# One state pair moved to another buffer, three products and one group of output evacuations moved to other places in the order (one core, Trainium2)

## The chip, the cores and the metric

The kernel runs on one core of a Trainium2 chip. A core has a matrix engine (PE, with its own weight-load stream PEld), a vector engine (DVE), a scalar engine (ACT), a general engine (POOL) and an engine that issues transfers (SP). Each takes its instructions in a fixed order and waits on semaphores for the others; transfers run beside them. The metric is the device time of one execution in microseconds (us), the median over several executions. The profile is one execution of its own, with every instruction's start and duration.

## The reference, cut to what matters

`x` is 2048 x 1024. Two branches are computed from it and mixed by a gate per row.

```
a  = S5 branch:  Bu = x B_bar^T (complex, 1024 states); h_t = Lam_bar h_(t-1) + Bu_t;  a = 2 Re(h C^T) + x Dskip
b  = H3 branch:  kv = shiftconv(k) * v;  y = FFT long convolution of kv with ssm_k;  b = x * (y + kv ssm_D)
g  = sigmoid(sum(x * gate_w))
out = g * a + (1 - g) * b
```

## The kernel before, in words

The work has two stages that overlap. In the first, about 215 us long, the convolution of the H3 branch is computed per chunk of 128 channels (eight chunks; loop `for c in range(NC - 1)` and then the last chunk, `c = 7`): tables and forward transforms on PE, products of spectra on DVE (`products`), the inverse on PE (`inverse`). Its results go to a scratch in HBM (`cv_scr`) and are read back by rows later (`loads`).

The second stage is the state recurrence. Time is cut into four blocks (`tb`) of 512 steps and the states into four groups (`g`) of 256. One pair `(tb, g)` is one item of the list `order`. For item `i`:

- `Bu(i)` makes two tiles on PE ("B12" in the plan means both tiles of item 12). ACT moves them from PSUM into a state buffer `U` (the half steps `V_` and `O_`), and writes first the carried end value into it (`U<-ends`).
- `turn_U` (the list `turns_U[i]`) multiplies one half by lambda on ACT (into `Q`), twice, and each time a POOL transfer that adds (`gather`, `U<-Q`) brings it into the other half. The second transfer of an item goes to the same place as the first.
- `scan(tb, g, ...)` is the recurrence on DVE: a front (two products with tables and two sums: `A<-TCS`, `trn<-TCS`, `A<-A,trn`), four scan instructions, then the products back (`U<-TCS,A`, `trn<-TCS,A`) and the join (`U<-U,trn`). Then the state is scaled by lambda, by ACT for the scans in `scaled_by_act = (4, 12, 13, 14)` (put into `put_off` and issued later as four `Q<-U`), by DVE else; the sums of scan j are woven between the scan instructions of scan j+1.

Outputs are made per row tile `k` (16 of 128 rows, four to a block): `Cy_row(k)` ("C0") or, for blocks 1 and 2, in groups: "G23" is group 3 of block 2, 32 matmuls, 8 for each of its four row tiles. Group 0 takes all four PSUM buffers, group 3 ends with `scale_a` (ACT, PSUM into SBUF, scaled by the gate) and `combine` (POOL transfer that adds the other branch). The last block (rows 12 to 15) takes the same four PSUM buffers again after them. `scale_b(k)` prepares the other branch of row `k`: two ACT passes, and a POOL transfer `pbb<-gd` (for some rows called `BT<-gd`, `BT<-BT` or `row<-gd`, after the buffer that they use). `product(k)` multiplies it with x on DVE, and waits for that transfer.

The order of everything is the order of the source text: `put` (L94) chains every instruction behind the previous one of its engine. The driver is the loop `for j in range(NS)` over the 16 scans: `advance(j)` runs scan j and weaves the front of scan j+1 into it; `between(j)` is called inside the scan, ahead of its scan instructions and again after them; then come `turned` (turns), `scaled_b`, and the units of `plan[j]`. All instructions have line L94 in the profile; the tile names tell them apart.

Buffers: `u4` is a pool of three buffers that serves temporaries early and the states 6, 7, 8 and 15 late. `fin` is a region at the right end of SBUF. It holds the temporary `t` of the last chunk's `products`, and was closed again when the last chunk's B tiles had been issued; the matrices `CT[4..7]` then took its place.

Of the kernel before, what the change touches and what calls it, by code (L numbers as in the profile page):

```python
# [11 lines left out]
BF16 = mybir.dt.bfloat16  # L12
# [8 lines left out]
def kernel(  # L21
# [46 lines left out]
    def pool(name, bufs, **kw):  # L68
        return ctx.enter_context(tc.tile_pool(name=name, bufs=bufs, **kw))
# [10 lines left out]
    s5p = {"wu": pool("wu", 3)}  # L80
# [5 lines left out]
    def ps2(shape, name):  # L86
        return psum.tile(shape, F32, name=name, tag="ps")
# [29 lines left out]
    def act(o, i, **kw):  # L117
        put("act", nc.scalar.activation, out=o, in_=i, **kw)

    def load_t(o, i):  # L120
        put("sp", nc.sync.dma_start_transpose, out=o, in_=i)
# [58 lines left out]
    def hold(column):  # L180
        act(column, pih, func=ACT.Copy)
# [74 lines left out]
    def load_xT(tb, halves=(0, 1), held=False):  # L256
        if tb == NTB - 1:
            xTs[tb] = BT[3].rearrange("p c d q -> p (c d q)").rearrange("p (d t) -> p d t", d=ND)
        elif tb not in xTs:
            xTs[tb] = (xt_pool if tb in (1, 2) else xt_first).tile([128, ND, TB], BF16, name="xT", tag="xT")  # L260
        for h in halves:
            if held:
                hold(xTs[tb][:, 0, h * HB:h * HB + 1])
            load_t(xTs[tb][:, :, h * HB:(h + 1) * HB], xf[tb * TB + h:(tb + 1) * TB:2, :])
# [502 lines left out]
    def inverse(c):  # L767

        G = whole.pop(c).rearrange("p (a c b f d) -> p a c b f d", a=2, c=2, b=4, d=128)
        for par in range(2):  # L770
            ps = ps2([128, 2, 4, 128], "psz")
            for j in range(2):
                tl = 2 * par + j
                for fi in range(2):
                    for cc, tab in enumerate((CI, SI)):
                        mm(ps[:, j], tab[:, fi, tl * 128:(tl + 1) * 128], G[:, par, 1 - cc, :, fi],
                           fi == 0 and cc == 0, fi == 1 and cc == 1)
            cv = cv_pool.tile([128, 2, 4, 128], BF16, name="cv")
            act(cv, ps, func=ACT.Copy)
            move(cv_scr[c, :, 2 * par:2 * par + 2], cv)  # L780
            yield
# [16 lines left out]
    def gate(tb):  # L798
        psg = ps2([128, 2, 512], "p")[:, 0, 0:4]
        for tl in range(4):  # L800
            for dt_ in range(ND):
                mm(psg[:, tl:tl + 1], xTs[tb][:, dt_, tl * 128:(tl + 1) * 128], gwb[:, dt_:dt_ + 1],
                   dt_ == 0, dt_ == ND - 1)
        gates_of(slice(tb * 4, tb * 4 + 4), psg)
# [28 lines left out]
    def Bu(i):  # L833
        tb, g = order[i]
        if i == 13:
            V_ = s5p["v13"].tile([128, 2, 2, HB], BF16, name="V13")
            O_ = lam_pool.tile([128, 2, 2, HB + 2], BF16, name="O13", tag="lamd")
            Us[tb, g] = V_, O_[:, :, :, 2:]
            turns_U[i] = turn_U(g, V_, O_)
            return [Bu_plain(tb, g, V_, O_, j) for j in range(2)]  # L840
        if i in (10, 11):
            if i == 10:
                s5p["u2"] = xt_pool.tile([128, 2, 2 * (4 * HB + 4)], BF16, name="U2", tag="xT")
            U = s5p["u2"][:, i - 10]
        else:
            shape = [128, 2 * (4 * HB + 4)]
            if i in (6, 7, 8, 15):
                U = u4(shape, BF16, "U")
            else:
                home = uu[0 if i in (0, 1, 14) else 1] if i < 6 or i == 14 else s5p["uu"]  # L850
                U = home.tile(shape, BF16, name="U")
        if i >= 2:
            V_, O_ = U[:, 0:4 * HB], U[:, 4 * HB:]
            V_ = V_.rearrange("p (c j t) -> p c j t", c=2, j=2)
            O_ = O_.rearrange("p (c j t) -> p c j t", c=2, j=2)
            Us[tb, g] = V_, O_[:, :, :, 2:]
            turns_U[i] = turn_U(g, V_, O_)
            return [(Bu_halves if i < 4 else Bu_plain)(tb, g, V_, O_, j) for j in range(2)]
        U = U[:, 0:8 * HB].rearrange("p (a c j t) -> p a c j t", a=2, c=2, j=2)
        Us[tb, g] = U[:, 0], U[:, 1]  # L860
        return [Bu_tile(tb, g, U, j) for j in range(2)]
# [24 lines left out]
    turns_U = {}  # L886
# [220 lines left out]
    def product(t_):  # L1107
        pbb, xr = ios[t_]
        tt(xr, xr, pbb, ALU.mult)
# [7 lines left out]
    def step(gen):  # L1117
        next(gen, None)

    def run(gen):  # L1120
        for _ in gen:
            pass

    def steps(gen, n):
        for _ in range(n):
            step(gen)
# [55 lines left out]
    old = none  # L1182
    parts = (None for i in range(4) for b in Bu(i) for _ in b)
    tiles = (b for i in (4, 5) for b in Bu(i))

    for c in range(NC - 1):
# [36 lines left out]
        tabs, back, prod = turn_table(c - 1) if c <= NG else none, inverse(c - 1), products(c)  # L1223
# [88 lines left out]
        old = tabs  # L1312

    h3r.close()
    c = NC - 1
# [34 lines left out]
    turning = [turn_C(pi) for pi in range(NP)]  # L1350
    load_CT(1)
    load_CT(2)
    load_CT(3)
    with tc.tile_pool(name="fin", bufs=1, side="right") as fin:

        count = iter(range(16))

        def room(shape, dt, name):
            return fin.tile(shape, dt, name=name, tag=f"fin{next(count)}")

        prod, back = products(c, 0, room, False), inverse(c - 1)
        run(old)
        steps(prod, 3)
        run(turns_U[3])
        run(next(tiles))
        steps(turning[0], 2)
        step(back)
        run(back)
        gate(1)
        gate(2)  # L1370
        steps(prod, 2)
        b6, b7 = Bu(6)
        run(b6)
        run(b7)
        run(turns_U[6])
        run(turning[0])
        run(prod)
        load_xT(3)
        b8, b9 = Bu(7)
        run(b8)  # L1380
        run(b9)
        run(turning[1])
        b10, b11 = Bu(8)
        run(b10)
        run(b11)
    back = inverse(c)
    step(back)
    run(back)
# [35 lines left out]
    def Cy(tb, tl):  # L1424
        ps = ps2([128, 2, 512], "psy")
        for g in range(NG):
# [4 lines left out]


    NS = NTB * NG
    plan = ["", "B9 B10", "B11", "B12 B13 C0", "C1", "C2", "C3 B14", "B15", "G10", "G11", "G12 G13", "G20", "G21 G22 G23",
            "", "", ""]
    turned = dict(zip(range(3, 12), (8, 9, 4, 10, 11, 12, 13, 14, 15)))
    turned[0] = 7
    multiplied = {4: (1,), 5: (2,), 6: (3,), 8: (4,), 9: (5,), 10: (6, 7), 11: (8,), 12: (9, 10)}
    loaded = {7: (7, 8), 8: (9, 10), 9: (11, 12), 10: (13,), 11: (14,), 12: (15,)}
    scaled_b = {1: (0,), 2: (1,), 5: (4,), 6: (5,), 8: (7, 8), 9: (9, 10), 10: (11,),  # L1440
                11: (12, 13), 12: (14,), 13: (15,)}
# [2 lines left out]
    def between(j):  # L1444
        for k in multiplied.get(j, ()):
            product(k)
        yield
        if j == 3:
            run(turning[6])
        if j == 12:  # L1450
            product(11)

    scans = [scan(j // NG, j % NG, between(j)) for j in range(NS)]

    def advance(j):
        step(scans[j])
        for k in range(3):
            if j + 1 < NS:
                step(scans[j + 1])
            step(scans[j])  # L1460
# [25 lines left out]
    for j in range(NS):  # L1486
        for k in loaded.get(j, ()):
            loads(k)
        if j == 7:
            store(3)  # L1490
        for k in stored.get(j, ()):
            store(k)
        advance(j)
        for t in turning[2 * j:2 * j + 2]:
            run(t)
        if j > 0:
            on_act += [lambda t=t: step(t) for t in turning[2 * j + 2:2 * j + 4] for _ in range(4 if j == 1 else 2)]
        turn = turns_U[turned[j]] if j in turned else none
        if j != 10 and plan[j][0:1] != "G":
            step(turn)  # L1500
        by_group = plan[j][0:1] == "G" and j != 10
        if j == 7:
            scale_b(6)
        if by_group:
            for n, k in enumerate(scaled_b.get(j, ())):
                if n == 1:
                    step(turn)
                scale_b(k)
            run(turn)
        if j == 4:  # L1510
            put_off.pop()()
            scale_b(3)
        for unit in plan[j].split():
            if unit == "C0":
                scale_b(2)
            if unit[0] == "G":
                Cy_group(int(unit[1]), int(unit[2]))
            else:
                (Bu_next if unit[0] == "B" else Cy_row)(int(unit[1:]))
        if put_off:  # L1520
            put_off.pop()()
        if j == 10:
            step(turn)
            for k in scaled_b[j]:
                scale_b(k)
            run(turn)
        elif not by_group:
            run(turn)
            if j == 5:
                run(turns_U[5])  # L1530
            for k in scaled_b.get(j, ()):
                scale_b(k)
        if j == 7:
            gate(3)
# [61 lines left out]
```

## Time and profile before

| | |
|---|---|
| median of 3 runs | 379.9 us (379.87 to 380.58) |
| the profiled execution, its own time | 381.04 us |
| its span, first to last instruction | 379.3 us |
| busy: PE, DVE, ACT, POOL | 369.9, 364.1, 307.6, 79.1 us |
| TensorE clock granted | full in every slice |
| DMA | 71.78 MB, mean 189 GB/s |

The rows of the timeline read: start, duration, engine, line, operation, output<-inputs, tile shape, how many instructions in a row were put together, and in brackets how long the engine had been idle before and what ended that. A `DMA` list gives issues of transfers with the time from issue to landing in its last column. Two cautions: a busy PE is a modelled span, and a wait for several semaphores is named after the one that came last.

### The profile page before, as it was taken

What the parts mean: (1) busy time and instruction counts of PE and PEld (TensorE: products, weight loads), DVE (VectorE), ACT (ScalarE), POOL (GpSimd) and SP (SyncE); (2) the same over time, 40 slices, a digit from 0 to 9 for tenths busy, and PEclk for the clock granted to TensorE, in tenths of its full rate; (3) what the DMA queues carried; (4) which work ended last, traced back from release to release, by engine and by line L of the source; (5) the groups of instructions that cost most, each with busy time, mean ns of one, the idle gap of its engine ahead of it and who ended that gap; (6) DMA issues with size and microseconds to landing.
All of it is one profiled execution on the core that took longest, in us unless ns stands there. A gap on an engine that the chain in (4) does not pass through costs nothing.

```text
span 379.3 us, 6647 instructions
## 1 busy us (share of the span) xinstructions
PE 369.9 (98%) x2434; PEld 200.3 (53%) x2469; DVE 364.1 (96%) x585; ACT 307.6 (81%) x473; POOL 79.1 (21%) x109
## 2 busy tenths in 40 slices
PE   7999999999999999999999999989999999999996
PEld 4656467575674847644544444434445444444444
DVE  8899999999999999999999999999999989969984
ACT  5879998988979899697949799998879868938501
POOL 4011030110301102021002012123443313635000
PEclk9999999999999999999999999999999999999999
DMA  7889999999999989968999999947998999998902
GB/s 168 168 114 264 215 213 189 236 218 203 228 200 185 215 166 194 179 145 153 207 183 209 215 186 253 256 101 131 197 247 138 251 247 204 160 255 146 221 0 111
DMA packets 126259, 71.78 MB, mean 189 GB/s; under 512 B 104649, under 2 KB 107601, under 8 KB 126226
## 3 DMA queue, kind: packets, MB, share of 16 engines
q1 hardware_dynamic: 112416, 45.90, 56.1%
q0 software_dynamic: 12688, 25.17, 38.7%
q10 hardware_dynamic: 1122, 0.28, 0.4%
q8 instruction: 19, 0.31, 0.3%
q14 instruction: 14, 0.11, 0.1%
HBM read 15.48 MB, written 8.39 MB: 63 GB/s over the span
## 4 chain that ended last, share of the span: by engine, by line
DVE 55%; PE 26%; issue 8%; DMA 5%; ACT 4%; POOL 0%; SPq 0%; POOLq 0%; DVEq 0%
PE psy L94 23%; DVE acc L94 20%; DVE wkh L94 13%; DVE A L94 5%; DVE Vh L94 4%; DVE t L94 3%; DVE U L94 2%; DVE ks L94 2%; DMA U<-Q 2%; ACT Q L94 2%; DVE trn L94 2%; PE taps L94 1%; DMA kT<-in_B_k_dram 1%; DMA BT<-gd 1%; DVE CT L94 1%
## 5 line engine op out<-in xcount | busy, mean ns | idle before, releaser
L94 PE MATMUL psy<-CT,U 128*128 128x512 bf16 (+1 forms) x418 | 92.7, 374 | 0.4
L94 PEld LDWEIGHTS <-U 128*128 128x128 bf16 x492 | 48.0, 98 | 57.3 <-issue 2.1
L94 PEld LDWEIGHTS <-BT 128*128 128x128 bf16 x544 | 50.5, 98 | 33.5 <-issue 0.2
L94 DVE TENSOR_TENSOR wkh<-BT,Vh 128x2048 bf16<-128x2048 bf16 (+3 forms) x31 | 44.6, 1457 | 0.0
L94 ACT ACTIVATE Q<-U,lam 128x512 bf16<-128x512 bf16 (+1 forms) x64 | 37.5, 632 | 8.5 <-DVE U L94 8.5
L94 POOL DMA_DIRECT2D U<-Q x26 | 26.6, 1033 | 82.9 <-ACT Q L94 42.4
L94 DVE TENSOR_TENSOR acc<-BT,Vh 128x4096 bf16<-128x4096 bf16 (+3 forms) x19 | 36.9, 1947 | 0.3 <-ACT Vh L94 0.2
L94 PE MATMUL both<-xT,BT 128*128 128x512 bf16 x157 | 35.2, 379 | 0.2
L94 ACT ACTIVATE Vh<-psv 128x1024 bf16<-128x1024 f32 x32 | 30.7, 1034 | 5.7 <-PE psv L94 5.6
L94 DVE TENSOR_TENSOR_SCAN A<-rv,init,A 128x256 bf16<-128x256 f32 x48 | 34.4, 738 | 0.0
L94 DVE TENSOR_TENSOR acc<-acc,wkh 128x1024 bf16<-128x1024 bf16 (+4 forms) x30 | 32.7, 1128 | 0.1
L94 ACT ACTIVATE U<-both 128x512 bf16<-128x512 f32 x44 | 24.2, 594 | 10.4 <-PE both L94 10.1
L94 ACT ACTIVATE BT<-psk 128x1024 bf16<-128x1024 f32 x31 | 30.0, 1035 | 2.3 <-PE psk L94 2.2
L94 POOL DMA_DIRECT2D acc<-wkh x8 | 9.7, 1218 | 100.7 <-DVE wkh L94 100.7
L94 PE MATMUL psk<-eok,SF 128*128 128x384 bf16 (+1 forms) x118 | 28.0, 354 | 0.2
L94 PEld LDWEIGHTS <-SF 128*128 128x128 bf16 x184 | 18.0, 98 | 19.1 <-issue 0.4
L94 PE MATMUL psz<-Vh,CI 128*128 128x512 bf16 x64 | 24.3, 379 | 0.0
L94 PE MATMUL psz<-Vh,SI 128*128 128x512 bf16 x64 | 24.3, 379 | 0.0
L94 PE MATMUL taps<-dg,kT 128*128 128x128 bf16 (+1 forms) x352 | 21.5, 208 | 1.0 <-DMA kT<-in_B_k_dram 1.0
L94 PEld LDWEIGHTS <-kT 128*128 128x128 bf16 x352 | 20.8, 99 | 2.5 <-DMA kT<-in_B_k_dram 2.0
L94 DVE TENSOR_TENSOR U<-U,trn 128x512 bf16<-128x512 bf16 (+1 forms) x58 | 21.2, 391 | 0.1
L94 PE MATMUL both<-xT,BTl 128*128 128x512 bf16 x94 | 21.1, 379 | 0.1
(223 smaller groups left out, 767.5 us busy)
## 6 DMA issues: line engine op xcount, KB each, us to landing
U<-Q POOLq DMA_DIRECT2D x26, 256.0 KB, 5.4
acc<-wkh POOLq DMA_DIRECT2D x6, 768.0 KB, 8.7
cv_scr<-cv SPq DMA_DIRECT2D x16, 256.0 KB, 4.8
kn<-in_B_ssm_k_dram SPq DMA_DIRECT2D x5, 512.0 KB, 3.7
v<-in_B_v_dram SPq DMA_DIRECT2D x5, 512.0 KB, 5.9
out_dram<-m SPq DMA_DIRECT2D x8, 256.0 KB, 4.8
BT<-cv_scr SPq DMA_DIRECT2D x7, 256.0 KB, 7.0
out_dram<-BT SPq DMA_DIRECT2D x7, 256.0 KB, 2.0
```

The costliest lines, as they stand in the source:

```text
L94: i = f(*a, **kw)
```

## The change

1. `fin` is no longer a block that is closed before the last inverse but a pool that stays, with one buffer under one tag, and `Bu(8)` takes its state buffer from it (`s5p["last"]`) instead of from `u4`. By the tiles' places in SBUF this has four consequences: state 8 uses the place that `t` had; `CT[4..7]` move by 4128 bytes and come to lie elsewhere than `t`; the room of row 11 (`row`) takes the `u4` buffer that state 6 had, not that of state 7; state 15 takes the third `u4` buffer, not that of state 6.
2. `product(4)`, `product(7)` and `product(11)` leave `between` and come after `advance(j)` for j = 8, 10, 12 (`behind`). On DVE they then stand after the front of scan j+1.
3. "G23" moves in the plan from j = 12 to j = 13. On PE no instruction moves, since nothing else of PE stands between. On ACT the four evacuations of rows 8 to 11 (`BT<-psy`) move behind `scale_b(15)` (`BT<-BT,omg` and `BT<-rows,gcols`) and behind the four `Q<-V` of scan 13. On POOL the transfer of row 15 comes ahead of the four transfers of rows 8 to 11. SP's order stays.

```diff
             shape = [128, 2 * (4 * HB + 4)]
-            if i in (6, 7, 8, 15):
+            if i == 8:
+                U = s5p["last"](shape, BF16, "U")
+            elif i in (6, 7, 15):
                 U = u4(shape, BF16, "U")
...
-    with tc.tile_pool(name="fin", bufs=1, side="right") as fin:
-
-        count = iter(range(16))
-
-        def room(shape, dt, name):
-            return fin.tile(shape, dt, name=name, tag=f"fin{next(count)}")
+    fin = pool("fin", 1, side="right")
+
+    def room(shape, dt, name):
+        return fin.tile(shape, dt, name=name, tag="fin")
+
+    s5p["last"] = room
...
-    plan = ["", "B9 B10", "B11", "B12 B13 C0", "C1", "C2", "C3 B14", "B15", "G10", "G11", "G12 G13", "G20", "G21 G22 G23",
-            "", "", ""]
+    plan = ["", "B9 B10", "B11", "B12 B13 C0", "C1", "C2", "C3 B14", "B15", "G10", "G11", "G12 G13", "G20", "G21 G22",
+            "G23", "", ""]
...
-    multiplied = {4: (1,), 5: (2,), 6: (3,), 8: (4,), 9: (5,), 10: (6, 7), 11: (8,), 12: (9, 10)}
+    multiplied = {4: (1,), 5: (2,), 6: (3,), 9: (5,), 10: (6,), 11: (8,), 12: (9, 10)}
+    behind = {8: 4, 10: 7, 12: 11}
...
         if j == 3:
             run(turning[6])
-        if j == 12:
-            product(11)
...
         advance(j)
+        if j in behind:
+            product(behind[j])
```

The lines between, from `prod, back = products(...)` to `run(b11)`, only lose one level of indentation.

More of the change, by code (lines that the diff above doesn't have):

```diff
@@ L1353 @@
     load_CT(3)
-    with tc.tile_pool(name="fin", bufs=1, side="right") as fin:
-        count = iter(range(16))
-        def room(shape, dt, name):
-            return fin.tile(shape, dt, name=name, tag=f"fin{next(count)}")
[L1361 to L1385, printed above, removed]
+    fin = pool("fin", 1, side="right")
+    def room(shape, dt, name):
+        return fin.tile(shape, dt, name=name, tag="fin")
+    s5p["last"] = room
+    prod, back = products(c, 0, room, False), inverse(c - 1)
+    run(old)
+    steps(prod, 3)
+    run(turns_U[3])
+    run(next(tiles))
+    steps(turning[0], 2)
+    step(back)
+    run(back)
+    gate(1)
+    gate(2)
+    steps(prod, 2)
+    b6, b7 = Bu(6)
+    run(b6)
+    run(b7)
+    run(turns_U[6])
+    run(turning[0])
+    run(prod)
+    load_xT(3)
+    b8, b9 = Bu(7)
+    run(b8)
+    run(b9)
+    run(turning[1])
+    b10, b11 = Bu(8)
+    run(b10)
+    run(b11)
     back = inverse(c)
```

## The prediction

> **What bounds the kernel now.** I read the page's busy times first, then the waits of each engine, then the timeline where a wait stands.
>
> ```profile
> PE 369.9 (98%) x2434; PEld 200.3 (53%) x2469; DVE 364.1 (96%) x585; ACT 307.6 (81%) x473; POOL 79.1 (21%) x109
> core 0: us, PE busy (x) PEld busy (x) DVE busy (x) ACT busy (x) POOL busy (x), PEclk, DMA share, GB/s
> 220.00:230.00 10.00, 9.95 (x47) 4.55 (x47) 9.93 (x23) 9.94 (x14) 1.11 (x2) 1.00 1.12 216
> 230.00:240.00 10.00, 9.95 (x47) 4.51 (x46) 10.00 (x23) 9.90 (x16) 3.73 (x5) 1.00 1.20 236
> 240.00:250.00 10.00, 8.76 (x40) 3.92 (x40) 9.90 (x25) 9.94 (x15) 1.83 (x3) 1.00 0.94 217
> 250.32 1.02 PE L94 MATMUL psy<-CTa,U 128*128 128x512 bf16 x4 [1.51 <-ACT U L94]
> ```
>
> PE is full, at full clock, and its rate sets the end. In the second stage it waits once: 1.51 us at 250.32, for ACT to empty the PSUM buffer that C0 needs. Between 220 and 250 ACT and DVE are full too. So a change can win at most that 1.5 us there, and lose wherever it makes PE wait anew. The rows of DVE and ACT matter through those two places.
>
> **The change, part 1: state 8 in the temporary's place.** The rows of ACT around the old place, and PE's first and last matmul of the last inverse:
>
> ```profile
> 208.93 1.13 ACT L94 ACTIVATE CT<-CT,mc2r 128x1024 bf16<-128x1024 bf16 x1
> 212.57 0.22 ACT L94 ACTIVATE U<-ends 128x4 bf16<-128x4 bf16 x1 [2.51 <-DMA U<-Q]
> 215.02 1.93 ACT L94 ACTIVATE cv<-psz 128x1024 bf16<-128x1024 f32 x2
> 216.83 0.73 ACT L94 ACTIVATE Q<-U,lam 128x512 bf16<-128x512 bf16 x1
> 213.90 0.38 PE L94 MATMUL psz<-Vh,SI 128*128 128x512 bf16 x1
> 200.43 1.29 DVE L94 TENSOR_TENSOR wkh<-wkh,t 128x1024 bf16<-128x1024 bf16 x2
> ```
>
> The first write of state 8 (`U<-ends`) waits 2.51 us because its buffer was the Q of item 6, which a transfer was still reading. In the new place it waits for the last read of `t`, over by 200.43 + 1.29 = 201.7: no wait, so it starts at 208.93 + 1.13 = 210.06. Not all of it lasts: the second `cv` needs the inverse's last matmul, 213.90 + 0.38 = 214.28; from its start to the Q of 216.83 is 0.90, so Q starts at 215.2 instead of 216.83: ACT leads by 1.6.
>
> ACT shows no idle time up to the wait of PE, so I let the lead reach it. The rows there:
>
> ```profile
> 245.63 3.19 PE L94 MATMUL both<-BT,BT 128*128 128x512 bf16 x13
> 249.19 2.06 ACT L94 ACTIVATE U<-both 128x512 bf16<-128x512 f32 x4
> ```
>
> The first two of the four `U<-both` end at about 250.25, with the lead at 248.65; PE is free at 245.63 + 3.19 = 248.82. The wait goes: PE **-1.5 us** from here. If the lead were lost to a late load on the way, it would be 0; both ends are kept.
>
> The other places cost nothing: `CT[4..7]` also wait for the last inverse matmul, but stand on SP behind the store of `cv`, which is later anyway; row 11's room waits for earlier matmuls than before, state 15 for a buffer long free.
>
> **Part 2: the three products.** DVE waits for the other branch's transfer at each:
>
> ```profile
> 289.58 0.69 DVE L94 TENSOR_TENSOR BT<-BT 128x1024 bf16<-128x1024 bf16 x1 [0.74 <-issue]
> 310.22 0.69 DVE L94 TENSOR_TENSOR xr<-xr,pbb 128x1024 bf16<-128x1024 bf16 x1 [1.31 <-DMA pbb<-gd]
> 334.05 0.40 DVE L94 TENSOR_TENSOR U<-U,trn 128x512 bf16<-128x512 bf16 x1
> 337.52 0.69 DVE L94 TENSOR_TENSOR row<-row 128x1024 bf16<-128x1024 bf16 x1 [3.07 <-issue]
> 338.13 0.68 DVE L94 TENSOR_TENSOR A<-TCS,V 128x1024 bf16<-128x1024 bf16 x1
> 341.88 1.39 DVE L94 TENSOR_TENSOR_SCAN A<-rv,init,A 128x256 bf16<-128x256 f32 x2
> 348.13 0.75 DVE L94 TENSOR_TENSOR V<-V,trn 128x512 bf16<-128x512 bf16 x2
> row<-gd POOLq DMA_DIRECT2D x1, 256.0 KB, 11.9
> 322.26 0.86 POOL L94 DMA_DIRECT2D V<-Q  x1 [6.38 <-ACT m L94]
> 325.55 2.87 POOL L94 DMA_DIRECT2D row<-gd  x1
> ```
>
> Products 4 and 7 move by a scan's length, far behind their transfers: -0.74 and -1.31, so DVE leads by 2.05 when it comes to 334.36 (the end of the 334.05 row, 0.31 on). Product 11 moves only behind 338.13 to 341.88, 3.75 us of work: DVE reaches it at 334.36 - 2.05 + 3.75 = 336.06. Its transfer landed at 325.55 + 11.9 = 337.45. So its wait shrinks but need not vanish; what is late next is this transfer.
>
> When does it land now? POOL's transfers of turns depend on one another: the second of an item waits for the first.
>
> ```profile
> 257.43 1.11 ACT L94 ACTIVATE m<-psy,gcols 128x1024 bf16<-128x1024 f32 x1 [2.07 <-PE psy L94]
> 260.03 3.16 ACT L94 ACTIVATE Q<-U,lam 128x512 bf16<-128x512 bf16 x5
> 259.63 0.75 DVE L94 TENSOR_TENSOR U<-U,trn 128x512 bf16<-128x512 bf16 x2
> 270.00 0.86 POOL L94 DMA_DIRECT2D U<-Q  x1 [0.34 <-DVE A L94]
> 325.02 2.52 POOL L94 DMA_DIRECT2D U<-Q  x1
> U<-Q POOLq DMA_DIRECT2D x1, 256.0 KB, 10.6
> 336.09 0.86 POOL L94 DMA_DIRECT2D U<-Q  x1 [7.67 <-ACT BT L94]
> ```
>
> The last two show a link: issued 325.02, landed 10.6 later (335.6), the next at 336.09. Such links run back to about 270. ACT moves with PE at 257.43 (-1.5), but the third of the Q's from 260.03 on belongs to scan 4, whose join ends at 259.63 + 0.75 = 260.38 whatever PE does; two Q's take 1.22, so it could start at 259.75 and starts at 260.46 instead of 261.25: -0.8. I take -0.8 for the chain and row 11's landing: 336.65. Ends: not moved (337.45), and before DVE arrives (336.06). One transfer more ahead of it costs 337.45 - 335.62 = 1.83 (these two land that far apart): 338.5.
>
> With 336.65: product at 336.72, scans of 13 at 336.72 + 0.61 = 337.33 instead of 341.88: DVE **-4.55**. Scan 13's join ends at 348.13 + 0.75 - 4.55 = 344.33.
>
> **Part 3: G23 a scan later.** PE's order is the same; ACT's isn't, and this adds a wait.
>
> ```profile
> 341.38 2.56 ACT L94 ACTIVATE Q<-U,lam 128x512 bf16<-128x512 bf16 x4 [5.76 <-DVE U L94]
> 343.84 2.09 ACT L94 ACTIVATE BT<-psy,gcols 128x1024 bf16<-128x1024 f32 x2
> 348.17 1.11 ACT L94 ACTIVATE BT<-psy,gcols 128x1024 bf16<-128x1024 f32 x1 [0.61 <-PE psy L94]
> 349.18 2.54 ACT L94 ACTIVATE Q<-V,lam 128x512 bf16<-128x512 bf16 x4
> 351.63 1.14 ACT L94 ACTIVATE BT<-BT,omg 128x1024 bf16<-128x1024 bf16 x1
> 333.02 0.99 SPq L94 DMA_DIRECT2D BT<-cv_scr  x1
> BT<-cv_scr SPq DMA_DIRECT2D x1, 256.0 KB, 7.0
> 347.97 1.03 PE L94 MATMUL psy<-CTa,U 128*128 128x512 bf16 x4
> 368.02 1.28 DVE L94 SCALAR_TENSOR_TENSOR BT<-psy,gcols,xlast 128x1024 bf16<-128x1024 f32 x1 [1.50 <-PE psy L94]
> ```
>
> Before, row 8 was out of PSUM by 344.9, three us ahead of block 3's first matmul (347.97), which takes that buffer. Now the four evacuations stand behind scan 13's four `Q<-V`, and these wait for the join. Queued behind them: rows 8 to 11's POOL transfers and stores, and PE. The walk: join 344.33, + 0.09 (a join at 341.29 released ACT at 341.38) = 344.42; four Q's 351.63 - 349.18 = 2.45: 346.87; row 8's evacuation 1.11: 347.98; PE 0.07 later (250.25 to 250.32): 348.05. PE alone would be there at 347.97 - 1.5 = 346.5: a **new wait of 1.6 us**, and block 3 starts 0.1 later than before. The next rows follow 1.04 apart, PE needs them 1.72 apart: no second wait. `scale_b(15)` hides: its load lands at 333.02 + 7.0 = 340.0, its two passes of about 1.04 end by 342.1, before the join. Row 11's evacuation ends some 1.8 later than 349.28; its transfer and store end far ahead of row 12's output (368.02 + 1.28). From 348 on PE runs through as before.
>
> Sum: -1.5 + 1.6 = **+0.1**. The profiled execution took 381.04 (span 379.3), 1.1 over the median of 379.9; on the median's scale 380.0. What counts in the end isn't PE's gain but when DVE's join comes: the sum moves one for one with row 11's landing.
>
> [...]
>
> **The rivals.**
>
> *Only the gain: 378.4.* PE keeps -1.5. For it: the wait at 250.32 is real. Against: the join of scan 13 would have to end by 342.7. DVE has no wait left beyond the 0.74 + 1.31 + 3.07 = 5.12, so 343.76 is the earliest. It needs shorter rows of DVE. Chance 0.08.
>
> *Row 11's transfer lands before DVE comes: 379.3.* Join at 343.76, block 3 at 347.5: -0.6. Against: the chain would have to move by 1.4. Chance 0.12.
>
> *Slower: the new wait outgrows the gain, 380.8.* If ACT's lead is lost before 249, or the transfers take longer, row 11 lands at 337.45 as before, the join is at 345.13 and block 3 starts 0.9 later; one transfer more ahead of it, in the moved chain, gives +1.9: 381.8. It decides from a landing after 337.3. For it: it takes no more than one link of the chain that comes out longer, or a lead that is used up. Chance 0.35.
>
> **How the numbers follow.** The forecast has 0.45. About 0.2% (0.76 us) is what a measurement of this kernel tells from no change. Forecast and second rival lie within it: same 0.57; faster 0.08; slower 0.35. The range takes in the early landing (379.3, and 0.1 for the spread of medians) and the late one (381.8): 379.2 to 381.8, leaving out the first rival and the far end of the third.
>
> **What would show it.** Right: no 2.51 idle before `U<-ends` near 210; no wait of PE near 249; DVE without idle time at products 4 and 7 and under 1 us at 11; a wait of PE of 1 to 2 us near 346.5 for `BT<-psy`, ahead of which ACT waits for DVE's V. Wrong: PE still waiting near 249 (lead lost); no wait near 346 (join earlier than DVE's rows allow); row 11 landing after 337.5.

## The result, and the profile after

The changed kernel takes 383.33 us (median of 9 executions, 381.29 to 387.37), the kernel before, run beside it, 379.77 (9 executions). The ratio is 1.0082, 95% interval 1.0061 to 1.0103: slower by some 3 us. Executions more than 1.5% above the fastest of the same kernel enter no ratio, and no median given below. The prediction was 380.0, with a range of 379.2 to 381.8. The profiled execution took 383.33 with a span of 381.6, against 381.04 and 379.3 before, so the two traces differ by 2.3 us. All times with two decimals below are from the traces' rows or from the end of the last instruction (379.25 and 381.56).

PE's waits of over 0.3 us in the changed kernel's second stage (what waited, what for, us in total, times, longest):

```profile
PE psy L94 <- ACT BT L94: 2.3, 1, 2.3
```

One wait, and it isn't the one of before: PE waited for `U` at C0, now it waits for row 8's evacuation at block 3. The timeline of ACT, then of DVE, then of PE, in the changed kernel:

```profile
209.67 0.20 ACT L94 ACTIVATE U<-ends 128x4 bf16<-128x4 bf16 x1
335.08 1.33 ACT L94 ACTIVATE Q<-U,lam 128x512 bf16<-128x512 bf16 x2 [1.38 <-DVE U L94]
339.03 1.33 ACT L94 ACTIVATE Q<-U,lam 128x512 bf16<-128x512 bf16 x2 [2.61 <-DMA U<-Q]
344.96 2.56 ACT L94 ACTIVATE Q<-V,lam 128x512 bf16<-128x512 bf16 x4 [2.52 <-DVE V L94]
347.43 4.09 ACT L94 ACTIVATE BT<-psy,gcols 128x1024 bf16<-128x1024 f32 x4
```

```profile
335.59 0.68 DVE L94 TENSOR_TENSOR row<-row 128x1024 bf16<-128x1024 bf16 x1
340.40 0.43 DVE L94 TENSOR_TENSOR U<-U,Q 128x512 bf16<-128x512 bf16 x1 [1.57 <-ACT Q L94]
344.12 0.75 DVE L94 TENSOR_TENSOR V<-V,trn 128x512 bf16<-128x512 bf16 x2
```

```profile
248.43 1.02 PE L94 MATMUL psy<-CTa,U 128*128 128x512 bf16 x4
348.57 1.40 PE L94 MATMUL psy<-CTa,U 128*128 128x512 bf16 x4 [2.34 <-ACT BT L94]
349.77 1.91 PE L94 MATMUL psy<-CT,U 128*128 128x512 bf16 x4
```

Up to C0 the changed kernel is ahead: no wait before `U<-ends`, no wait at C0, which starts at 248.43 instead of 250.32. Product 11 doesn't wait at all. Then two things cost. In the lists of POOL's issues and of its transfers (KB each, us from issue to landing):

```profile
323.35 2.36 POOL L94 DMA_DIRECT2D row<-gd  x1
333.98 0.86 POOL L94 DMA_DIRECT2D U<-Q  x1 [8.26 <-DMA out_dram<-m]
```

```profile
row<-gd POOLq DMA_DIRECT2D x1, 256.0 KB, 11.6
```

Row 11's transfer lands at 334.95. The `U<-Q` of 333.98 is state 14's second; it takes 5.0 us to land, until 338.98. On ACT, the second pair of scan 12's `Q<-U` waits 2.61 us, until 339.03, for a Q buffer, which that transfer is still reading. DVE waits 1.57 us for that pair, and scan 13's join ends at 344.12 + 0.75 = 344.87. Behind it stand the four `Q<-V`, then row 8's evacuation, then block 3: PE is idle for 2.34 us.

And the matmuls of 348.57 are slower: four to 1.40 us, later 1.91, where four had taken 1.02. Stretches of 3.41 us around the wait show the clock with them (columns: stretch, its length, busy us and number of instructions on PE, its weight loads, DVE, ACT and POOL, granted TensorE clock, DMA share, GB/s):

```profile
342.25:345.67 3.42, 3.42 (x18) 1.53 (x17) 3.42 (x9) 0.90 (x3) 2.42 (x3) 1.00 0.69 115
345.67:349.08 3.41, 1.07 (x6) 0.43 (x5) 3.41 (x7) 3.41 (x6) 0.27 (x1) 1.00 0.69 119
349.08:352.49 3.41, 3.41 (x10) 1.19 (x9) 3.41 (x8) 2.44 (x3) 2.98 (x4) 0.50 0.70 120
352.49:355.91 3.42, 3.37 (x17) 1.51 (x16) 3.42 (x8) 2.56 (x4) 0.18 (x1) 1.00 1.08 223
```

From 349.08 on, for 3.41 us, PE is granted half its clock (0.50): 10 matmuls, where the stretches from 342.25 and from 352.49, at full clock and without the wait, have 18 and 17. Half of 3.41 is 1.7 us lost.

The account between the two traces, by PE alone:

| | before | after | difference |
|---|---|---|---|
| last matmul of the last inverse starts | 213.90 | 213.60 | -0.30 |
| from there to C0's first matmul | 36.42 | 34.83 | -1.59 |
| C0 to block 3's first matmul | 97.65 | 100.14 | +2.49 |
| block 3's first matmul to the end | 31.28 | 32.99 | +1.71 |
| end | 379.25 | 381.56 | +2.31 |

The wait counts as 2.34 in its row and as 2.49 in the table, because a matmul's modelled end lies about 0.16 behind the point where the next would have started. The same 0.16 comes back in f3 below: its stretch of 130.48 is 1.55 over 128.93, its wait 1.39. Below I use the stretch from C0's first matmul to the end. It is 128.93 us before (97.65 + 31.28) and 133.13 after, and it leaves out the first stage, which differs by up to 4.4 us between these traces (the last inverse's last matmul lies between 213.15 and 217.52).

### The profile page after: what moved, and what is told of

It is laid out like the page before. It is cut to its first block, busy times and chain, and to the rows that moved or that the text cites. A ratio compares the mean times of both kernels' runs of the same rounds, so it can differ in the third digit from the quotient of the medians.

```text
span 381.6 us, 6644 instructions
## 1 busy us (share of the span) xinstructions
PE 371.4 (97%) x2434; PEld 200.6 (53%) x2469; DVE 364.0 (95%) x585; ACT 307.7 (81%) x473; POOL 79.4 (21%) x109
## 4 chain that ended last, share of the span: by engine, by line
DVE 57%; issue 14%; DMA 12%; PE 11%; ACT 3%; POOL 2%; SPq 0%; POOLq 0%; DVEq 0%; ACTq 0%
DVE acc L94 20%; DVE wkh L94 12%; PE psy L94 8%; DMA U<-Q 6%; DVE A L94 6%; DVE Vh L94 4%; DVE U L94 3%; DVE t L94 3%; DVE trn L94 3%; DVE ks L94 2%; ACT Q L94 2%; DMA out_dram<-m 2%; DMA m<-xr 2%; PE taps L94 1%; DMA kT<-in_B_k_dram 1%
```

## The experiments

| run | edit | PE's wait at block 3 | half clock | C0 to end | ratio to before, 95% |
|---|---|---|---|---|---|
| after (first trace) | | 2.34 | 3.41 | 133.13 | 1.0082 [1.0061, 1.0103] |
| f3_changed | none | 1.39 | 0 | 130.48 | 1.0050 [1.0013, 1.0086] |
| e1_group_back, f2_group_back | parts 1 and 2 | 0, 0 | 0, 0 | 128.93, 128.94 | 1.0004 [0.9969, 1.0039], 0.9994 [0.9965, 1.0022] |
| e2_group_alone | part 3 | 4.08 | 6.83 | 135.86 | 1.0099 [1.0053, 1.0145] |
| e3_room_alone | part 1 | 0 | 0 | 128.92 | 0.9984 [0.9948, 1.0019] |
| e4_products_alone | part 2 | 0 | 0 | 128.93 | 0.9993 [0.9964, 1.0022] |
| e5_evac_first, f1_evac_first | after, `Q<-V` behind the evacuations | 0, 0 | 0, 0 | 128.92, 128.93 | 0.9979 [0.9951, 1.0007], 0.9991 [0.9961, 1.0021] |
| e6_five_q | after, five Q buffers | 0.74 | 0 | 129.85 | 0.9991 [0.9956, 1.0027] |
| e7_filled | after, PE's wait filled | 1.13 | 0 | 132.38 | 1.0045 [1.0017, 1.0074] |
| e8_back_five_q | parts 1, 2, five Q | 0 | 0 (3.41 at C0) | 130.26 | 0.9978 [0.9947, 1.0009] |

"Half clock" is the time at half clock between C0 and the last stretch of matmuls (half clock at the very end is left out: in e4 the mean clock from 360 to 380 is 0.95, and the stretch is 128.93 all the same). In the traces of e2, e3 and e8 ACT waits for loads of `CT` (3.69 to 5.72 us the longest) and C0 starts at 259.60, 255.86 and 254.80, later than in all the others (247.98 to 252.35); of these three I use only what lies from C0 on, and the clock.

**Which part costs.** Parts 1 and 2 together, and each part alone.

```diff
-    plan = [..., "G20", "G21 G22",
-            "G23", "", ""]
+    plan = [..., "G20", "G21 G22 G23",
+            "", "", ""]
```

This is e1, against the changed kernel. e2 is the kernel before with the same lines changed the other way; e3 is the kernel before with the edits of `Bu` and `fin` alone; e4 is the kernel before with those of `multiplied`, `behind` and `product` alone.

> The changed kernel with G23 put back to scan 12, so parts 1 and 2 alone. Theory A (the loss is all in part 3: the evacuations behind scan 13's Q<-V make PE wait 2.34 us before block 3, and the half clock after it costs another 1.7): PE has no wait of over 0.3 us after 215, the clock stays full, and the time is 1.5 us under the kernel before, about 378.3, ratio 0.996. Rival B (part 1 or 2 costs time by itself, by the moved CT tiles or by transfers that collide): the time stays above the kernel before, 380.5 to 383. Rival C (the wait at 250 hid no real loss, PE only waits elsewhere): 379.8, ratio 1.000, with a new wait of about 1.5 us in the trace.

> The kernel before with part 3 alone (G23 at scan 13). Theory A: scan 13's join ends at 348.9 as before, so block 3 can start only 3.7 us later (0.09 + 2.45 for four Q + 1.11 for row 8 + 0.07), at 352.6 instead of 347.97: a PE wait of 4.6 us, then a stretch of half clock of about 3.4 us (+1.7): the time is 6.3 us over the kernel before, about 386.1. If the half clock has nothing to do with PE's wait: 384.4, at full clock. Rival B (part 3 isn't the loser): within 1 us of the kernel before.

> The kernel before with part 1 alone (state 8 in the temporary's room). Theory A: the 2.51 us of ACT before U<-ends and PE's 1.51 us at 250 are gone, nothing else changes: 1.5 us under the kernel before, about 378.3. Rival B (part 1 costs): 380.5 or more. Rival C (the gain is lost further on): 379.8, with a new wait of PE of about 1.5 us.

> The kernel before with part 2 alone (products 4, 7, 11 behind). Theory A: DVE's waits of 0.74, 1.31 and most of 3.07 go and scan 13's join comes about 4 us earlier, but PE, which sets the end, waits for nothing of it, and its 1.51 us at 250 stay: within 0.4 us of the kernel before (379.4 to 380.2). Rival B (part 2 costs, since a later product holds up a combine or a state): 380.8 or more. Rival C (DVE, at 96% busy, is a second bound): 1 to 4 us under the kernel before.

Block 3's first matmul and the span in e1, then in e2, then three stretches of e2:

```profile
core 0 of [0], span 381.0 us
349.75 1.03 PE L94 MATMUL psy<-CTa,U 128*128 128x512 bf16 x4
```

```profile
361.49 1.01 PE L94 MATMUL psy<-CTa,U 128*128 128x512 bf16 x2 [4.08 <-ACT BT L94]
```

```profile
356.68:360.09 3.41, 0.73 (x4) 0.21 (x3) 3.41 (x8) 2.21 (x4) 0.00 (x0) 1.00 0.91 156
360.09:363.50 3.41, 2.01 (x5) 0.69 (x5) 3.41 (x8) 3.41 (x5) 1.63 (x2) 0.50 0.11 20
363.50:366.91 3.41, 3.41 (x9) 1.18 (x8) 3.41 (x9) 2.37 (x4) 1.80 (x3) 0.50 1.04 182
```

The traces of e1 and e2 agree with theory A behind C0: without part 3 there is no wait; with part 3 alone there is one of 4.08 (expected 4.6), and the half clock lasts 6.83 us (360.09 to 366.91). In e2 the stretch grows by 6.93 us (expected 6.3). Its executions are 4.4 us slower by the medians (386.1 against 381.7). This is less than the trace says: three of the eight behind that median have a mean clock of 1.000, so no half clock came in them. Parts 1 and 2 do not show the 1.5 us in the time: e1, e3 and e4 can't be told from the kernel before. For e1 and e3 this misses theory A's 378.3. That is not a loss behind C0, since their stretch is 128.9. In e3's trace it lies ahead of it: `U<-ends` doesn't wait, as expected, but PE waits 2.83 us at C0 all the same, which e3's theory A had as gone. f4 below takes this up. For e4 theory A's "no change" came true. Its wait before product 11 is 0.30 us, where the prediction's walk, for all three parts together, has 0.66 (336.72 less 336.06):

```profile
250.44 1.02 PE L94 MATMUL psy<-CTa,U 128*128 128x512 bf16 x4
336.66 0.69 DVE L94 TENSOR_TENSOR row<-row 128x1024 bf16<-128x1024 bf16 x1 [0.30 <-issue]
```

The first row says something else too: C0 of e4 has no wait, although part 1 isn't in it.

**Place or order?** In `e5` G23 stays at scan 13, and only the `Q<-V` go behind the evacuations:

```diff
             if g == NG - 1:
-                if tb == 2 and tl == 0:
-                    put_off.pop()()
                 scale_a(k, [(slice(0, D), flat(ps))])
```

> The changed kernel with one thing else: G23 stays at scan 13, but the four Q<-V of scan 13 are issued behind the evacuations of rows 8 to 11, not ahead of row 8's. Measured by the stretch from C0's first matmul to the end of the span, which is 128.93 us in every trace without a PE wait behind it, and 133.13 in the changed kernel. Theory A (the loss is the evacuations behind Q<-V and the join, plus the half clock that follows PE's wait): no PE wait at block 3, full clock, stretch 128.9, and a time like that of parts 1 and 2 alone. Rival B (the later place of G23 in the text costs by POOL's order, row 15's transfer ahead of those of rows 8 to 11): the stretch stays above 131.

ACT in e5, then block 3's first matmul:

```profile
341.70 2.09 ACT L94 ACTIVATE BT<-psy,gcols 128x1024 bf16<-128x1024 f32 x2
346.83 2.55 ACT L94 ACTIVATE Q<-V,lam 128x512 bf16<-128x512 bf16 x4
345.61 1.03 PE L94 MATMUL psy<-CTa,U 128*128 128x512 bf16 x4
```

Row 8 is out at 342.8 and block 3 starts at 345.61 without a wait: stretch 128.92. POOL's transfers keep the changed kernel's order in it. So it isn't the plan's scan, nor POOL's order, but that four `Q<-V`, and with them the wait for scan 13's join, stood ahead of the evacuations on ACT.

**The Q buffer.**

```diff
-    s5p["Q"] = pool("Q", 4)
+    s5p["Q"] = pool("Q", 5)
```

> The changed kernel with five Q buffers instead of four. Theory A (my sum missed that scan 12's second pair of Q waits 2.61 us for a Q buffer that state 14's second transfer still reads, and DVE waits 1.57 us for it): that wait and the 1.57 go, scan 13's join ends 1.57 earlier, block 3 waits 0.8 us instead of 2.34. If the half clock needs a PE wait longer than the 1.51 us that the kernel before had at full clock, the clock stays full: stretch from C0's first matmul to the end 128.93 + 0.8 = 129.7. Rival B (the half clock comes with any wait at this place): 131.4. Rival C (not the buffer but the join sets it): 133.1, wait still 2.3.

ACT's `Q<-U` of scan 12, DVE's join of scan 13 and block 3 in e6:

```profile
336.46 2.56 ACT L94 ACTIVATE Q<-U,lam 128x512 bf16<-128x512 bf16 x4 [1.45 <-issue]
343.82 0.75 DVE L94 TENSOR_TENSOR V<-V,trn 128x512 bf16<-128x512 bf16 x2
348.27 1.02 PE L94 MATMUL psy<-CTa,U 128*128 128x512 bf16 x4 [0.74 <-ACT BT L94]
```

The four `Q<-U` go through in a row. Counted from C0 (249.72 in e6, 248.43 after), the join starts at 94.10 instead of 95.69: 1.59 earlier, as DVE's wait of 1.57 was. PE waits 0.74 (expected 0.8) at full clock, the stretch is 129.85 (expected 129.7). Theory A holds, rivals B and C fall. `e8` asks whether the fifth buffer is of use without part 3:

> Parts 1 and 2 (G23 back at scan 12) with five Q buffers. If PE alone sets the end where it never waits, the fifth buffer buys nothing: stretch from C0's first matmul to the end 128.93 as with four, and the time that of parts 1 and 2 alone (the fastest runs 0.3 to 1.5 us under those of the kernel before). Rival: DVE's or ACT's shorter waits bring the last block forward: 127 to 128.5.

It isn't: 130.26 is 128.93 and 1.33, and 1.37 is what the half clock adds there (of the 3.41 us at half clock from 254.13 on, in which a wait of 4.92 us at C0 ends, PE is busy for 2.74, twice 1.37). No shorter stretch than 128.92 was seen in any run.

**The half clock.** `e7` gives PE work in place of its wait, without making block 3 able to start any earlier: ten matmuls whose weights are zero, added to row 11's sums, which they leave as they are.

```diff
+    zero = pool("zero", 1).tile([128, 128], BF16, name="zero")
+    nc.gpsimd.memset(zero, 0.0)
...
+            if (tb, g, tl) == (2, NG - 1, 3):
+                for n in range(10):
+                    mm(ps[:, n % 2], zero, CT[6][:, 0, 0:512], False, False)
             Cy_g(tb, tl, [ps[:, 0], ps[:, 1]], g, g == NG - 1)
```

> The changed kernel with ten more matmuls (128x512, weights of zero, added to row 11's sums, so that the result stays) at the head of row 11's share of G23: 10 x 0.216 = 2.2 us of work for PE, in place of its wait. Block 3 can start no earlier, since row 8's evacuation ends as late as before. Theory A (the half clock follows from PE's idle time): PE's wait is about 0.2 us, the clock stays full, block 3 starts where it did, and the stretch from C0's first matmul to the end is 133.13 - 1.69 = 131.4, though PE has 2.2 us more to do. Rival B (the half clock has another cause, the load or the time since the start): half clock all the same, stretch 133.1. Rival C (PE wasn't waiting, added matmuls are added time): 135.3.

PE, DVE and one ACT row of e7:

```profile
345.23 2.32 PE L94 MATMUL psy<-CT,zero 128*128 128x512 bf16 x10
347.39 1.89 PE L94 MATMUL psy<-CT,U 128*128 128x512 bf16 x8
350.41 1.02 PE L94 MATMUL psy<-CTa,U 128*128 128x512 bf16 x4 [1.13 <-ACT BT L94]
```

```profile
342.23 0.43 DVE L94 TENSOR_TENSOR U<-U,Q 128x512 bf16<-128x512 bf16 x1 [2.57 <-ACT Q L94]
```

```profile
340.87 1.33 ACT L94 ACTIVATE Q<-U,lam 128x512 bf16<-128x512 bf16 x2 [3.60 <-DMA U<-Q]
```

The clock stays full (1.00 from 346.08 to 352.90) with 2.16 us more of matmuls (347.39 less 345.23), and from block 3's first matmul to the end it is 31.28 us, as before the change. The stretch is 132.38, not 131.4: in this execution the transfer that holds the Q buffer landed later (ACT waits 3.60 instead of 2.61, DVE 2.57 instead of 1.57), so block 3 started 0.96 later. Without the ten, PE's wait would have been 3.29 us by my estimate (1.13 and 2.16); in the changed kernel the half clock came with 2.34. No run shows this execution without the ten, so it is an inference from the two traces that they kept the clock full; the last section has a wait of 2.83 us with which it stayed full without any. Rival B's half clock and 133.1 didn't come, nor rival C's 135.3. In the time as a whole e7 can't be told from the changed kernel: its ratio to the kernel before is 1.0045, that of f3 1.0050.

**Once more, on one chip.**

> The changed kernel with Q<-V behind the evacuations, once more and with more executions. Its trace had no PE wait in the second stage; the stretch from C0's first matmul to the end should be 128.9 again. If the wait at 250 of the kernel before is there in most executions, the time is 1.5 us under it, ratio 0.996. If the first stage varies by more than that wait, so that PE often comes to C0 later than ACT, the gain is smaller: 0.3 to 1 us, ratio 0.997 to 0.999.

> Parts 1 and 2 with G23 at scan 12, once more. Stretch from C0's first matmul to the end 128.9; the same time as with Q<-V behind the evacuations, within 0.5 us, since neither has a PE wait there.

> The changed kernel itself, on the same chip as the two kernels without PE's wait. [...]

> The kernel before, for a second profile. If ACT's chain before C0 (the wait for the transfer U<-Q ahead of U<-ends) sets C0's start and not PE, C0 starts near 250.3 whatever the first stage took: from the last inverse's last matmul to C0 it is 34.83 us where PE comes late (214.9 or later, as with the products alone, 215.61) and more, up to 36.4, where it comes early (213.9). Rival: the 1.51 us are there always, 36.4 us.

Block 3 in f3, and C0 and ACT's row ahead of it in f4:

```profile
348.15 1.02 PE L94 MATMUL psy<-CTa,U 128*128 128x512 bf16 x4 [1.39 <-ACT BT L94]
```

```profile
251.18 1.02 PE L94 MATMUL psy<-CTa,U 128*128 128x512 bf16 x4 [2.52 <-ACT U L94]
```

```profile
209.82 0.20 ACT L94 ACTIVATE U<-ends 128x4 bf16<-128x4 bf16 x1
225.89 2.19 ACT L94 ACTIVATE Q<-CT,mc2i 128x1024 bf16<-128x1024 bf16 x2 [2.50 <-DMA CT<-in_A_C_im_dram]
```

The two kernels without the wait at block 3 agree (medians 380.7 and 380.6), and the changed kernel is 2.3 us over them (383.0). Its wait was 1.39 this time, at full clock (1.00 from 344.41 to 351.23), against 2.34 in the first trace: the transfer landed earlier (ACT waited 2.05 for the Q buffer, DVE 1.01), and DVE came to product 11 0.38 us earlier, counted from C0. Of the nine executions behind its median four have a mean clock of 0.994 to 0.996 (3.41 us at half is 1.7 of 381 us, 0.0045), median 384.2; the five others have 381.7. That is 3.5 and 1.0 us over the two kernels, less than the 4.2 and 2.5 that the first two traces give with and without the half clock (2.49 + 1.71, and 2.49). Of those without the wait, one of twelve (f1) and two of eleven (f2) have such a clock, f2's profiled one from a wait in the first stage. By the two traces the half clock at block 3 comes in some executions of the changed kernel and not in others; the mean clocks fit this, though they don't say where in an execution it was half. What a wait of 2 us or more does to the clock, f3 with its 1.39 doesn't test; two traces in the last section do.

In f4 both expectations for the kernel before missed: C0 starts 37.43 us behind the last inverse's last matmul. Its `U<-ends` doesn't wait, yet PE waits 2.52 us at C0, because ACT waited 2.50 us for the load of `CT`. In e4, with the same code there, neither wait shows and C0 has none. So the wait at C0 that part 1 was to remove is 1.51, 2.52 or 0 us, by which transfer lands late in an execution, and part 1 removes only one of its two causes. The other is seen with part 1 in place too: in e3 and e8 ACT waits 3.69 and 4.59 us for a load of `CT`, and PE 2.83 and 4.92 at C0. This would explain why parts 1 and 2 gain less than 1.5 us on the median (0.7 to 0.8 us under the kernel before in f1 and f2, which the intervals don't tell from zero); how often each wait comes wasn't counted. No kernel here beats the kernel before by more than its uncertainty. f1 and f2, the kernels of e5 and e1, are 2.3 us under the changed kernel by the medians on the same chip, though the intervals of their ratios just touch its own (up to 1.0022, from 1.0013).

## Why the prediction was wrong

- **Part 1, `U<-ends` and C0: right for the traces compared, too sure for the median.** No idle before `U<-ends` at 209.67, C0 without a wait, -1.59 for -1.5. What I took for a constant of the kernel was one late transfer of one execution (f4, e4).
- **Part 2: right.** The DVE waits at products 4, 7 and 11 are gone, and the time doesn't follow (e4). Row 11's transfer landed at 334.95, 1.7 us before my 336.65: I moved the chain of transfers by 0.8, it moved by 2.5 (337.45 before); why by so much, no run shows.
- **Part 3, the walk to block 3: the term "new wait of 1.6 us" was mis-sized, and this is the first step that failed.** Its mechanism is what happened (join, four Q, row 8's evacuation, 0.07), and each of those durations held. The join's time didn't: 344.87 instead of 344.33. DVE came to product 11 at 335.59, 1.13 before my 336.72, but then lost 1.57 at scan 12's sums, because ACT's second pair of `Q<-U` waited 2.61 us for a Q buffer. I had followed row 11's transfer to its landing but not `U<-Q` of state 14, POOL's next issue, and I moved all of DVE's rows behind product 11 together, as if the sums of scan 12 among them waited for nothing. The trace before had the price: there this transfer, issued at 336.09, took 5.7 us to land, so even 0.8 earlier it frees the buffer at 341.0. ACT, released by scan 12's join (moved to about 335.4) and done with the first pair 1.24 later, would have wanted it at about 336.7. e6 confirms the wait for the buffer, by one edit that frees it. With PE free 0.3 earlier than predicted, the wait was 2.34. It is no constant either: f3 has 1.39, below the 1.6, and e7 would have had 3.3 without its ten matmuls, by the estimate above.
- **The sentence "From 348 on PE runs through as before": wrong, and the larger error.** It is 1.7 us of half clock that no term or rival had. The profile before showed full clock in every slice with a wait of 1.51 us in it; I took that to hold for any wait of this size, though it said nothing of longer ones. Here the wait was 2.34 us, and the clock was half from 349.08, 0.51 behind its end.
- **The rivals.** The slower one had the right direction and place and ended at 381.8, with a late landing of row 11 as its cause. Row 11 landed early; the late transfer was another, and the clock came on top: an end near 381.8 would have been luck. The second rival is at -0.5 by its own numbers (347.48 for 347.97), so 379.4 and not 379.3. And 343.76 wasn't the earliest join: without DVE's 1.57 it would have ended at 343.30; 0.3 of the difference is that the changed trace runs 0.3 ahead from the first stage on. With both terms put right the sum for these two traces is -0.3 - 1.6 + 2.5 + 1.7 = +2.3.
- **What stays open.** The first comparison's medians differ by 3.6 us, and its interval allows 2.3 to 3.9; the trace pair explains 2.3, e7 shows that the Q buffer's wait alone can add 1 us more. On one chip (f1 to f3 and the kernel before beside them) the medians give a gain of 0.7 to 0.8 for parts 1 and 2 and a loss of 2.3 for part 3, +1.6 in all, where the prediction has 1.5, 1.6 and +0.1. How often each happens, these runs don't say.

## What to carry to other kernels

Behind a change of order, walk every instruction that comes to stand ahead of an evacuation back to all it waits for, the buffer that it writes included, and not only its input. Where the sum leaves PE idle, ask what the clock does after it: in the kernel before it stayed full with a wait of 1.51 us, in the changed kernel it was half for 3.41 us with one of 2.34. Work for PE in that place saves only the half clock (block 3 to the end took 31.28 us in e7, 32.99 in the first trace); a shorter queue ahead of the evacuation saves the wait too (C0 to the end 128.92 in e5, 133.13 in the first trace: 4.2 together). A wait for a transfer that stands in one trace is a sample: before a change is to remove it, see in a second trace whether it is there.

## What the runs showed of the hardware

In these traces the length of PE's wait alone doesn't tell the clock that follows. Stretches of 3.41 us, columns as above: in e3, where PE waits 2.83 us at C0, and in f2, where it is without a matmul for 2.18 us in the first stage (3.41 less 1.23):

```profile
251.60:255.01 3.41, 1.43 (x7) 0.56 (x6) 3.38 (x12) 3.38 (x6) 0.99 (x2) 1.00 0.69 173
255.01:258.42 3.41, 2.56 (x12) 1.17 (x12) 3.38 (x8) 3.41 (x9) 0.72 (x1) 1.00 0.92 159
```

```profile
148.43:151.84 3.41, 1.23 (x36) 1.08 (x35) 3.41 (x5) 1.36 (x3) 0.86 (x1) 1.00 1.00 261
151.84:155.25 3.41, 3.41 (x45) 2.92 (x42) 3.41 (x5) 2.23 (x4) 0.00 (x0) 0.50 1.06 198
```

With the longer wait the clock stayed full (e3: 1.98 us of it lies in the first stretch and 0.85 in the second, both at 1.00); with the shorter one it was half for the next 3.41 us (f2: 0.50 from 151.84 on). In the 3.41 us ahead of their half clock PE was busy for 1.07 us in the changed kernel and for 0.73 in e2, whose half clock lasted 6.83 us. What makes the difference between e3 and f2, no run was made to show.

The second thing is how unevenly the transfers land that add into a buffer: the same Q buffer came free so that ACT waited 2.05, 2.61 or 3.60 us (f3, the changed kernel, e7), and PE's wait at block 3 followed from 1.39 us to 2.34 (0.56 of that by DVE's wait for the buffer), and in e7, by estimate, to 3.3 without the filling (1.13 + 2.16).
